# Another written-out order for a fused linear attention and squared-ReLU feed-forward kernel

## The chip, the cores and the metric

The kernel runs on one core of one Trainium2 chip. The metric is the time of one execution on the device in microseconds (us). Three runs of the kernel before gave 346.32, 346.35 and 348.3 us; their median is 346.35 us. Lower is better.

The core has five engines with queues of their own: PE (matmul; its weight loads are shown as PEld), DVE (vector), ACT (scalar, with the exponentials), POOL (here it issues the loads) and SP (here it issues transposes by DMA, and stores). Each works through its instructions strictly in the order in which the program lists them, so an instruction that waits holds up all that stand behind it on its engine.

## The reference

Two stages. The first is a linear attention with a feature map made of two exponentials, for 8 batches of 8 heads, 576 positions and 64 channels:

```python
def phi(x):
    proj = np.einsum('bhsd,df->bhsf', x, w_phi)
    proj = proj - np.max(np.abs(proj), axis=-1, keepdims=True)
    return np.concatenate([np.exp(proj), np.exp(-proj)], axis=-1)
q_p, k_p = (phi(q), phi(k))
kv = np.einsum('bhsf,bhsd->bhfd', k_p, v)
z = np.sum(k_p, axis=2)
num = np.einsum('bhsf,bhfd->bhsd', q_p, kv)
den = np.einsum('bhsf,bhf->bhs', q_p, z)[..., None] + 1e-06
return (num / den).astype(np.float32)
```

The second takes the result as 4608 tokens of 512 features, with w_in of 512x2048 and w_out of 2048x512:

```python
h = np.maximum(x @ w_in, 0.0)
return (h * h @ w_out).astype(np.float32)
```

## The kernel before, in words

The program first makes a list of 1741 operations (`add`, from line 60), each with an engine, a function that emits its instructions, and what it reads and writes. An operation is named here by its number in that list and its short name, as in 989:Xxk. Nothing of the list depends on the constants that the change touches.

For a batch b the operations are these. Loads of k, q and v by POOL (`xk` at L254, `xq` at L283, `xqr` at L274, `xv`; the last 64 positions at L262 as `xks`, `xqs`, `xvs`). Transposes of k and q: for batches 0 and 1 by PE (`Txk`, `Txq`, L325) with a copy out of PSUM (`Cxk`, `Cxq`), from batch 2 on by one DMA each from SP's queue (`Xxk`, `Xxq`, L336). The projection by w_phi in groups (`Pk`, `Pq`, L352, for batch 0 L379 and L501; `Fq`, L579, gives it the other way round). These have a contraction of 64 rows, so that two of them stand in the upper and lower half of PE's array at once; the list marks them `tiled`, and all other work of PE uses the full array. Then the greatest absolute value (`Mk`, `Mq`, on DVE), two exponentials (`Ekp`, `Ekn`, `Eqp`, `Eqn`, on ACT), the scaling of v (`em` on ACT, `V`, `V4` on DVE), `KV` on PE (L465, L470) and its copy `kvc`. For batches 3 to 7 the features of q are made row-wise and transposed by a DMA from SP (`Xf`, L558). The output of the attention for 128 positions is `NA`, a scaling `SA` on DVE, `NB` (L658), a reciprocal `rd` and a product `xo`; for the first 128 positions the same is done in two halves (`NAh`, `SAh`, `NBh`, `rdh`, `xoh`). It is transposed by PE for batch 0 (`Tx`, `Txh`, with the copies `Cx`, `Cxh`) and by a DMA from SP after that (`Xx`, L718).

The feed-forward works on chunks of 512 tokens. `F1` (L804; for the first chunk in smaller pieces at L815, L829 and L843) makes 4 matmuls of 128x512 into one PSUM bank, `relu` takes it out (on ACT at L781 or on DVE at L783), `sq` squares it (L790), `F2` (L898) makes 4 matmuls of 128x512 of a sum over 16, and `ot` copies the result, which SP stores. The last 128 tokens go in two parts (L862, `last_out`). The feed-forward of one chunk is mixed with the attention of the batches that come after it.

What sets the order is written out by hand in constants at the end of the file:

- `ORDER` (from L983) is a permutation of the 1741 operations. Each engine emits its own of them in this order; `pin` (L136) ties every instruction to the one before it on its engine.
- `STATES` gives one bit for each operation that can run on ACT or on DVE: the `relu`, `ot` and `kvc` operations and the copies of the transposes by PE.
- `BASES` gives the PSUM bank (0 to 7) of each of the 380 uses of a bank. A use waits until the one before it in the same bank has been read out.
- `GATES` names, for each load from batch 2 on, an operation of another engine that must have ended before the load is issued.
- `FILL` puts matmuls of zeros (128 wide, L977) ahead of some operations of PE in the first microseconds; nothing reads what they write.

The lines that use the constants:

```python
        if now[0].seq in GATES:
            dep(i, plan.ops[GATES[now[0].seq]].ins, mybir.DependencyClass.Sync)
...
        for op in self.ops:
            if op.alt is not None and STATES[op.group] == "1":
                op.eng, op.occ, op.lat = op.alt
        for g, b in zip(self.banks, BASES):
            g.base = int(b)
        return [self.ops[i] for i in ORDER]
...
            bank, n = FILL[op.seq]
            for _ in range(n):
                pin(nc.tensor.matmul(out=psum[:, bank, :P], lhsT=warm, rhs=warm, start=True, stop=True))
```

Of the kernel before, what the change touches and what calls it, by code (L numbers as in the profile page):

```python
# [108 lines left out]
def kernel(  # L109
# [964 lines left out]
)  # L1074
STATES = (
    '0101000100010000111100000010110000000010000000010101011000000001000000001111001000100000000001010000'
    '0100011000010000010000000000000101001010001101000001000100101000100111111000000100000010011010011111'
    '110001011000011111011110110100100'
)
GATES = {  # L1080
# [46 lines left out]
```

## Time and profile before

| what | value |
| --- | --- |
| three runs | 346.32, 346.35, 348.3 us (median 346.35) |
| the profiled execution's own time | 345.83 us |
| its span, first to last instruction | 344.0 us |
| granted PE clock | 1.000 |
| busy: PE, DVE, ACT, POOL | 335.8, 269.8, 231.3, 95.6 us |
| matmuls (fillers among them) | 3301 (91) |
| moved by DMA | 51.51 MB |

The span is 1.83 us shorter than the execution's own time, and that time is 0.52 us under the median of the three runs. In the busy shares a matmul counts from its start to a modelled end, and matmuls overlap: a 128x512 matmul is given as 379 ns, while a row of 16 of them ends 3.45 us after it began, which is 0.216 us from start to start. So PE's busy time says where PE stood still for long, and the starts of its matmuls say how well it was filled. "x8" in a line of the timeline means that eight instructions of a kind were merged into it; the first figure is the start, the second the length, and what stands in brackets is the idle time before it and what ended that.

### The profile page before, as it was taken

How to read it: one execution, taken by the hardware profiler on the slowest of the kernel's cores; microseconds unless marked ns; L12 is line 12 of the kernel's file. 1: busy time of each engine (PE TensorE's matmuls, PEld its weight loads, DVE VectorE, ACT ScalarE, POOL GpSimd, SP SyncE). 2: the span in 40 equal slices, each digit the busy share in tenths (PEclk: the TensorE clock that was granted, in tenths of full speed). 3: DMA queues.
4: the chain of work that ended last, by engine and by line, in shares of the span. 5: the costliest groups of instructions: out<-in, count | busy, mean ns of one | idle time of the engine just before them, and what ended most of it. 6: DMA issues, size and time to landing. Idle time of an engine off the chain costs nothing.

```text
span 344.0 us, 8335 instructions
## 1 busy us (share of the span) xinstructions
PE 335.8 (98%) x3301; PEld 188.8 (55%) x3301; DVE 269.8 (78%) x519; ACT 231.3 (67%) x436; POOL 95.6 (28%) x143
## 2 busy tenths in 40 slices
PE   8799999999999999999999999999999999999995
PEld 7678866545544555546545654455565444444443
DVE  5999998899899988798979897897996546863431
ACT  5999987699979798686888987977566402220120
POOL 8738360854620660104604060330000000000000
PEclk9999999999999999999999999999999999999999
DMA  9999999998999999999999999998864922000115
GB/s 130 176 203 195 202 172 164 159 160 166 163 178 214 179 163 232 163 191 183 158 211 142 216 169 215 162 157 183 162 125 105 158 82 71 0 2 35 56 37 149
DMA packets 142935, 51.51 MB, mean 150 GB/s; under 512 B 111472, under 2 KB 138416, under 8 KB 142896
## 3 DMA queue, kind: packets, MB, share of 16 engines
q1 hardware_dynamic: 97488, 32.35, 50.0%
q0 software_dynamic: 44960, 18.23, 48.4%
q8 instruction: 26, 0.43, 0.5%
q10 hardware_dynamic: 448, 0.39, 0.4%
q14 instruction: 13, 0.11, 0.1%
HBM read 36.73 MB, written 9.44 MB: 134 GB/s over the span
## 4 chain that ended last, share of the span: by engine, by line
PE 87%; ACT 5%; DMA 3%; DVE 1%; issue 1%; POOL 1%; SPq 1%; POOLq 0%; DVEq 0%; ACTq 0%
PE psum L898 34%; PE psum L804 30%; PE psum L658 6%; PE psum L352 5%; PE psum L465 4%; PE psum L843 2%; DMA kT<-xk 2%; ACT kn L394 1%; PE psum L829 1%; PE psum L815 1%; ACT qpn L594 1%; PE psum L862 1%; ACT kp L394 1%; DMA xT<-xo 1%; PE psum L470 1%
## 5 line engine op out<-in xcount | busy, mean ns | idle before, releaser
L898 PE MATMUL psum<-wout,h 128*128 128x512 bf16 x560 | 133.2, 379 | 0.0
L804 PE MATMUL psum<-xT,win 128*128 128x512 bf16 x448 | 105.3, 379 | 0.3 <-DMA xT<-xo 0.3
L781 ACT ACTIVATE hr<-psum 128x512 bf16<-128x512 f32 x104 | 60.4, 603 | 57.2 <-PE psum L804 45.2
L898 PEld LDWEIGHTS <-h 128*128 128x128 bf16 x560 | 50.8, 98 | 54.9 <-issue 0.5
L804 PEld LDWEIGHTS <-win 128*128 128x128 bf16 x512 | 47.6, 98 | 53.4 <-DMA xT<-xo 0.8
L790 DVE TENSOR_TENSOR h<-hr 128x512 bf16<-128x512 bf16 x144 | 56.6, 414 | 10.7 <-ACT hr L781 10.3
L554 ACT ACTIVATE qf<-psum 128x1024 bf16<-128x1024 f32 (+1 forms) x50 | 46.1, 938 | 13.8 <-PE psum L352 11.3
L405 DVE TENSOR_REDUCE mk<-psum 128x8 f32<-128x1024 f32 (+1 forms) x35 | 38.7, 1111 | 4.6 <-ACT kp L411 2.7
L783 DVE TENSOR_SCALAR hr<-psum 128x512 bf16<-128x512 f32 x40 | 26.9, 684 | 13.7 <-PE psum L804 13.1
L411 ACT ACTIVATE kn<-psum 128x1024 bf16<-128x1024 f32 (+1 forms) x35 | 32.7, 939 | 5.9 <-PE psum L352 4.2
L411 ACT ACTIVATE kp<-psum 128x1024 bf16<-128x1024 f32 (+1 forms) x35 | 32.9, 940 | 4.1 <-PE psum L352 2.4
L274 POOL DMA_DIRECT2D xq<-in_q_dram x24 | 17.4, 728 | 64.3 <-ACT hr L781 12.0
L670 DVE TENSOR_TENSOR psum<-psum,en 128x520 f32<-128x520 f32 (+1 forms) x39 | 27.4, 702 | 9.2 <-PE psum L658 5.5
L658 PEld LDWEIGHTS <-qpn 128*128 128x128 bf16 x624 | 27.2, 98 | 13.3 <-issue 1.4
L437 DVE TENSOR_TENSOR va<-xv,va 64x256 bf16<-64x256 bf16 (+2 forms) x66 | 29.8, 472 | 2.0 <-ACT va L429 1.1
L658 PE MATMUL psum<-kv,qpn 128*128 128x65 bf16 x624 | 30.4, 193 | 0.1
L541 DVE TENSOR_REDUCE mq<-psum 128x8 f32<-128x1024 f32 (+1 forms) x25 | 27.7, 1109 | 2.7 <-ACT qf L554 2.4
L594 ACT ACTIVATE qpn<-psum 128x1024 bf16<-128x1024 f32 (+1 forms) x30 | 27.2, 942 | 2.0 <-PE psum L579 1.1
L254 POOL DMA_DIRECT2D xk<-in_k_dram x27 | 19.9, 738 | 31.1 <-ACT hr L781 15.9
L684 DVE TENSOR_TENSOR xo<-psum,rden 128x512 bf16<-128x512 f32 (+1 forms) x39 | 26.6, 685 | 0.9 <-DMA xT<-xo 0.3
L254 POOL DMA_DIRECT2D xv<-in_v_dram x27 | 19.8, 741 | 14.4 <-PE psum L658 10.0
L195 ACT ACTIVATE ot<-psum 128x512 f32<-128x512 f32 x20 | 12.0, 598 | 12.8 <-PE psum L898 12.7
(81 smaller groups left out, 379.8 us busy)
## 6 DMA issues: line engine op xcount, KB each, us to landing
out_dram<-ot SPq DMA_DIRECT2D x32, 256.0 KB, 3.0
xk<-in_k_dram POOLq DMA_DIRECT2D x25, 128.0 KB, 5.9
xq<-in_q_dram POOLq DMA_DIRECT2D x24, 128.0 KB, 4.2
xv<-in_v_dram POOLq DMA_DIRECT2D x24, 128.0 KB, 4.9
win<-in_moe_w_in_dram POOLq DMA_DIRECT2D x4, 512.0 KB, 10.4
wout<-in_moe_w_out_dram POOLq DMA_DIRECT2D x4, 512.0 KB, 10.3
xq<-in_q_dram POOLq DMA_DIRECT2D x4, 256.0 KB, 5.9
out_dram<-ot SPq DMA_DIRECT2D x6, 128.0 KB, 2.6
```

The source lines that it names most:

```text
L254: pin(nc.gpsimd.dma_start(out=x[:, a * 512 : z * 512].rearrange("p (h x) -> p h x", x=4 * D), in_=src[b][2 * a : 2 * z, 0:512, :].rearrang ...
L405: pin(nc.vector.tensor_reduce(out=mk_view(g), in_=ps2(pj)[:, :, : n * Fd].rearrange("p e (i f) -> p e i f", f=Fd), axis=AX.X, op=ALU.max, ...
L411: pin(nc.scalar.activation(out=dst[slot][:, :, :n, :].rearrange("p e i f -> p e (i f)"), in_=ps2(pj)[:, :, : n * Fd], func=ACT.Exp, scale= ...
L437: pin(nc.vector.tensor_tensor(out=t[:, :, :D].rearrange("p m (x c) -> p m x c", c=2), in0=x.rearrange("p (m x c) -> p m x c", m=n, c=2), i ...
L541: pin(nc.vector.tensor_reduce(out=mqb[:, c, :, :n], in_=ps2(pj)[:, :, : n * Fd].rearrange("p e (i f) -> p e i f", f=Fd), axis=AX.X, op=ALU ...
L554: pin(nc.scalar.activation(out=o, in_=i_, func=ACT.Exp, scale=sgn))
L594: pin(nc.scalar.activation(out=o, in_=i_, func=ACT.Exp, scale=sgn))
L658: pin(nc.tensor.matmul(out=o[:, u // 4, u % 4 * D1 : (u % 4 + 1) * D1], lhsT=qpn[slot][:, sg * half + u * m : sg * half + u * m + P], rhs= ...
L781: pin(nc.scalar.activation(out=hr[sl], in_=ps1(g), func=ACT.Relu))
L790: pin(nc.vector.tensor_tensor(out=dst, in0=i_, in1=i_, op=ALU.mult))
L804: pin(nc.tensor.matmul(out=o, lhsT=win[mc // 4][:, kc, mc % 4 * P : (mc % 4 + 1) * P], rhs=x, start=(kc == 0), stop=(kc == KC - 1)))
L898: pin(nc.tensor.matmul(out=ps1(g), lhsT=h2[c % 2][mc // 4][:, mc % 4, tt * P : (tt + 1) * P], rhs=wout[mc // 4][:, mc % 4, :], start=(mc = ...
```

## The change

The five constants are replaced; not one operation is added, removed or altered, and every function of the program stays as it is. Cut to the lines that are spoken of (the first number of a line of `ORDER` has no meaning; the two lists are cut at other places by the line length alone):

```diff
 ORDER = [
-    2, 0, 6, 5, 8, 1, 7, 17, 10, 23, 13, 3, 4, 11, 15, 12, 16, 44, 45, 14, 46, 18, 49, 47, 77, 88, 48, 78, 20, 89,
-    50, 79, 52, 22, 90, 83, 85, 21, 94, 96, 51, 19, 84, 91, 53, 66, 30, 92, 113, 80, 54, 32, 82, 67, 55, 114, 95, 24,
...
-    345, 216, 183, 350, 397, 173, 217, 184, 174, 185, 383, 205, 218, 340, 346, 351, 189, 341, 190, 206, 186, 342,
...
-    302, 520, 280, 398, 202, 257, 303, 521, 273, 283, 258, 274, 295, 281, 269, 255, 284, 526, 256, 275, 285, 399,
...
-    307, 379, 315, 308, 548, 316, 309, 584, 317, 400, 404, 403, 552, 392, 406, 401, 318, 322, 556, 420, 395, 323,
...
-    499, 731, 540, 493, 656, 494, 749, 495, 626, 459, 655, 628, 753, 500, 618, 657, 620, 622, 609, 754, 665, 621,
-    623, 501, 612, 735, 502, 503, 611, 710, 666, 773, 714, 625, 736, 793, 610, 668, 706, 627, 667, 677, 702, 707,
...
-    964, 826, 697, 950, 827, 907, 842, 951, 698, 908, 968, 699, 700, 862, 969, 874, 828, 916, 877, 909, 989, 903,
-    875, 911, 904, 830, 843, 925, 876, 832, 905, 899, 701, 865, 829, 912, 939, 831, 926, 864, 833, 917, 900, 866,
-    913, 921, 863, 929, 922, 901, 927, 855, 867, 918, 886, 1367, 923, 991, 970, 947, 930, 993, 985, 934, 940, 992,
...
+    2, 0, 1, 17, 12, 6, 7, 5, 15, 23, 3, 9, 11, 16, 10, 4, 14, 44, 45, 13, 46, 18, 49, 47, 88, 77, 48, 89, 22, 78,
+    90, 52, 20, 51, 79, 96, 30, 95, 66, 85, 83, 113, 21, 53, 93, 91, 19, 50, 80, 92, 34, 114, 54, 8, 84, 67, 55, 25,
...
+    212, 223, 358, 268, 389, 377, 252, 244, 251, 383, 259, 224, 512, 361, 247, 388, 249, 372, 250, 301, 292, 254,
+    593, 302, 362, 248, 253, 516, 363, 261, 272, 303, 201, 391, 367, 520, 262, 398, 386, 293, 202, 257, 378, 387,
...
+    276, 319, 392, 306, 277, 320, 544, 321, 399, 534, 307, 278, 370, 282, 281, 308, 313, 400, 314, 538, 401, 315,
...
+    600, 653, 599, 495, 731, 654, 458, 604, 499, 735, 792, 626, 500, 620, 656, 745, 624, 628, 655, 501, 736, 749,
+    502, 622, 503, 657, 609, 665, 610, 753, 668, 720, 754, 633, 612, 621, 724, 666, 719, 1170, 611, 706, 1168, 635,
...
+    813, 825, 698, 950, 821, 831, 815, 699, 830, 843, 700, 862, 951, 989, 874, 863, 907, 876, 903, 833, 877, 832,
+    911, 864, 908, 952, 929, 820, 701, 904, 819, 912, 917, 865, 913, 970, 899, 855, 875, 866, 921, 900, 909, 905,
+    930, 925, 901, 922, 918, 826, 926, 990, 931, 886, 991, 927, 834, 992, 828, 827, 1014, 994, 923, 836, 867, 835,
...
 BASES = (
-    '4646164041135252302126010200212463200564360250721353062204415777202261022550062627452774740476572002'
...
+    '3027061374341562122716452046650406464142600425321445456663272342324066466020444001720131014535316624'
...
 STATES = (
-    '0101000100010000111100000010110000000010000000010101011000000001000000001111001000100000000001010000'
...
+    '0101010000000000100001010101000000000000000001100100011000100010010000001000001101110000100101110100'
...
 GATES = {
-    380: 186, 381: 90, 382: 144, 383: 53, 384: 344, 385: 119, 386: 93, 387: 361, 388: 44, 389: 65, 390: 339, 391: 67,
...
+    380: 184, 381: 194, 382: 228, 383: 371, 384: 197, 385: 149, 386: 218, 387: 248, 388: 91, 389: 359, 390: 340,
...
 FILL = {
-    44: (0, 26), 46: (0, 6), 79: (0, 2), 53: (0, 21), 55: (7, 6), 68: (7, 4), 109: (7, 3), 119: (7, 13),
-    150: (5, 10),
+    44: (0, 26), 46: (0, 8), 88: (1, 3), 90: (5, 4), 79: (7, 3), 66: (7, 2), 55: (0, 9), 119: (4, 15), 175: (4, 2),
+    147: (3, 9), 122: (2, 2), 129: (2, 3), 164: (7, 3),
 }
```

Counted over the whole of both lists: of the `relu` operations 40 run on DVE before and 43 after, of the `ot` 15 and 14, of the `kvc` 14 and 13, of the copies of transposes of k and q 13 and 14; the others run on ACT. Fillers are 91 before and 89 after. In the list of PE's operations, two neighbours of which one is `tiled` and the other isn't stand 106 times before and 96 times after.

More of the change, by code (lines that the diff above doesn't have):

```diff
@@ L983 @@
 ORDER = [
[84 rows of a table removed]
[84 rows of a table added]
 ]
 BASES = (
-    '4646164041135252302126010200212463200564360250721353062204415777202261022550062627452774740476572002'
-    '2234050406562660306644747744515564044733360014606323030002065257723721523632167404444060644135642622'
-    '2411755603017321744466422012226426662113311032101300001014426622554324066124147766101100154152402636'
-    '46617631044214100632037002065360056746106374667253600175114302553045653704562301'
+    '3027061374341562122716452046650406464142600425321445456663272342324066466020444001720131014535316624'
+    '4520364044000426664070736120063336252744040462213026664622422123033100210163010444200415230026066377'
+    '7545641626501273542622036766404000606044212567775273246764206432626002404400220011211063002331736464'
+    '65454024020022027334724675357666454352233772216364547742253770443765767176405332'
 )
 STATES = (
-    '0101000100010000111100000010110000000010000000010101011000000001000000001111001000100000000001010000'
-    '0100011000010000010000000000000101001010001101000001000100101000100111111000000100000010011010011111'
-    '110001011000011111011110110100100'
+    '0101010000000000100001010101000000000000000001100100011000100010010000001000001101110000100101110100'
+    '1101000000000001111000010010010100000001011100000000010001001001001101001000100001011000001011011000'
+    '111100101010101110001100001011001'
 )
 GATES = {
[11 rows of a table removed]
[11 rows of a table added]
 }
 FILL = {
-    44: (0, 26), 46: (0, 6), 79: (0, 2), 53: (0, 21), 55: (7, 6), 68: (7, 4), 109: (7, 3), 119: (7, 13),
-    150: (5, 10),
+    44: (0, 26), 46: (0, 8), 88: (1, 3), 90: (5, 4), 79: (7, 3), 66: (7, 2), 55: (0, 9), 119: (4, 15), 175: (4, 2),
+    147: (3, 9), 122: (2, 2), 129: (2, 3), 164: (7, 3),
 }
```

168 rows, old and new, of tables (GATES, ORDER) are left out of this document.

## The prediction

> **What bounds the kernel now.** I read the page's busy shares and slices first, then busy time by stretches, then PE's waits, and last the timeline where PE waits or changes its kind of work. From the page:
>
> ```profile
> PE 335.8 (98%) x3301; PEld 188.8 (55%) x3301; DVE 269.8 (78%) x519; ACT 231.3 (67%) x436; POOL 95.6 (28%) x143
> ...
> PE   8799999999999999999999999999999999999995
> ...
> DVE  5999998899899988798979897897996546863431
> ACT  5999987699979798686888987977566402220120
> ...
> q8 instruction: 26, 0.43, 0.5%
> ```
>
> PE is the bound from the second slice on; DVE and ACT are as full as PE only in the first slices. By stretches (span, then busy time of PE, PEld, DVE, ACT, POOL, then granted clock and DMA):
>
> ```profile
> 0.00:27.00 27.00, 23.07 (x348) 18.40 (x349) 23.01 (x56) 22.70 (x51) 17.57 (x29) 1.00 1.31 171
> 27.00:45.00 18.00, 17.98 (x292) 15.51 (x290) 17.22 (x34) 17.26 (x35) 10.28 (x15) 1.00 1.39 198
> 45.00:245.00 200.00, 199.48 (x2052) 107.97 (x2050) 174.16 (x320) 161.65 (x300) 67.73 (x100) 1.00 1.24 178
> 245.00:344.00 99.00, 95.27 (x616) 46.89 (x614) 55.45 (x112) 29.68 (x54) 0.00 (x0) 1.00 0.33 78
> ```
>
> Standing still, PE loses 3.93 us before 27 us, 0.5 us from there to 245 us, and 3.7 us at the end, where the last copy and store follow the last matmul. Of the waits after the head, two are on DMAs:
>
> ```profile
> PE psum L804 <- DMA xT<-xo: 0.3, 1, 0.3
> ...
> PE psum L352 <- DMA kT<-xk: 0.2, 1, 0.2
> ```
>
> These are understated, since a matmul is shown busy past its streaming. From start to start it is more:
>
> ```profile
> 107.87 0.59 PE L804 MATMUL psum<-xT,win 128*128 128x512 bf16 x2
> ...
> 108.79 0.39 PE L804 MATMUL psum<-xT,win 128*128 128x512 bf16 x1 [0.32 <-DMA xT<-xo]
> ```
>
> Two matmuls begin at 107.87 and, 0.22 later, 108.09; the third should follow at 108.30 and begins at 108.79, 0.49 late. In the same way the `Pk` at 154.07 us, which waits for kT, is 0.33 late.
>
> Last, what a change of kind costs PE:
>
> ```profile
> 68.69 1.04 PE L898 MATMUL psum<-wout,h 128*128 128x512 bf16 x4
> 69.66 0.40 PE L352 MATMUL psum<-wphi,qT 64*128 64x128 bf16 x8
> 69.89 0.38 PE L579 MATMUL psum<-qT,wphi 64*128 64x512 bf16 x2
> 70.14 0.40 PE L352 MATMUL psum<-wphi,qT 64*128 64x128 bf16 x8
> 70.47 0.39 PE L804 MATMUL psum<-xT,win 128*128 128x512 bf16 x1
> ```
>
> Four `F2` matmuls take 4 x 0.216 = 0.86 us, but from 68.69 to the half-array matmuls at 69.66 pass 0.97. Eight of those take 0.23 when half-array work follows (69.66 to 69.89) and 0.33 when full-array work does (70.14 to 70.47). So each passage between the kinds costs about 0.10 us, both ways, and no row of waits shows it.
>
> With starts, the whole sum closes: the useful matmuls at their spacing (0.216 us for 512 wide, 0.109 for 256, 0.056 for 128, 0.029 for 65, half that for half-array pairs) make 313 us. The first useful one starts at 4.1 us, the last at 340.05. The 23 us between are 106 passages (10 us), some 10 us of fillers and waiting up to 27 us, and some 3 us of small delays after that, 2.8 of them from 45 to 245 us.
>
> **The change part by part.** The sum is made against the profiled execution's 345.83 us (span 344.0, and 1.83 around it).
>
> Passages: 106 become 96. Ten at 0.10 us make -1.0 us. Every one lies on PE's own row, where nothing covers it. The order of `Pk`, `Pq` and `Fq` decides alone, so I take the whole; 0 and -1.0 are the ends.
>
> The Trainium skill ("TensorE: Matmul & The Clock Gate", Part 2, step 1) says that PE pulls the loading of the next weights ahead of matmuls in flight when their row groups don't conflict or they go to the background buffer. Read alone, that would hide the passage and make this term 0, which is a rival below. The 0.10 us at 69.66 and 70.47 speak against it.
>
> The two DMA waits. I laid the useful matmuls at their spacing, plus passages, between an operation's place in ORDER and its first user on PE. From 495:Xx to the first `F1` of its chunk (710 before, 720 after) lie 2.6 us of PE work before and 5.4 after. It landed 3.3 us after its issue, so the wait of 0.49 is gone. From 989:Xxk to 991:Pk it is 7.1 before and 8.0 after; the 0.9 more exceed the 0.33 that it came late. The other transposes keep a least distance of 4.6 us for `Xx` (2.6 before), 7.0 for `Xf` (6.5) and 8.0 for `Xxk` (7.1). What is late next is 1476:Xx (4.6, landing after 2.4) and 885:Xx (4.9, landing after 3.1), both with room. I take -0.8; ends -0.8 and 0.
>
> The head, which is PE's place only in name. From 5.9 to 25 us DVE's instructions follow each other without a gap over 0.12 us, and ACT's too; PE waits for them. ACT has the same load ahead of the last `kvc` before the output (132): copies 110 and 208 leave it, 78 and 226 come, of the same size. On DVE, ahead of 144:xoh, four copies of kT go (three of 128x512 at 415 ns, one of 128x256 at 273, each starting some 0.08 before the one before has ended: 1.2 us) and two copies of qT and a memset (410, 410, 278 ns: 0.95) come, -0.25. But between 144 and the copies `Cxh` that give the feed-forward its first input now stand 118 and 210, +0.5. So `Cxh` (25.73 and 25.94) ends some 0.3 later. PE meanwhile does `Pq`, `Fq` and `Pk` (1.1 us) that it did around the first `F1` pieces anyway, so only part of the delay reaches it. The start is bound by the landing of k at 3.70 us (ACT's cast) and 5.97 us (the load that is issued first in both), so the earlier identity on POOL gains nothing. I take +0.2. Ends: -1.0, about a third of the 2.9 us that PE idles there after its first filler, and +0.9, the 1.2 us that DVE would lose if the moved copies waited for PE as 45 and 47 did (0.89 and 0.85 idle), less 0.3.
>
> Fillers: 91 become 89, in time in which PE waits for DVE and ACT; 0. If that cover is gone they cost 89 x 0.056 = 5 us, as now.
>
> Engines: three more `relu` on DVE (684 ns; ACT 603), one `ot` and one `kvc` fewer, one copy more, about +1.4 us on DVE and as much less on ACT. DVE idles 25.8 us between 45 and 245; 0, at worst +0.5 in the head's last part.
>
> Banks, other small delays: banks are used again no sooner than before (0.86 us of PE work after the matmul that filled them, in both, outside the head); before, such waits cost 0.15 to 0.18 each, four times. 0; ends -0.5 and +1.0. The last operations of PE and the stores stand in the same order: 0.
>
> Loads on POOL: the second block of keys is issued after as much data as before (8.3 MB, 8.5 before, by the sizes of the page's list of DMA issues), but planned later; 0, with its danger below.
>
> Sum: 345.83 - 1.0 - 0.8 + 0.2 = 344.2. The median of the runs stood 0.5 over the profiled time, so 344.7 us, 1.6 us or 0.5% under 346.35. A measurement of this kernel tells about 1% (3.5 us) from no change.
>
> **The rivals.**
>
> Slower: the keys come late. 383:xk, a quarter of batch 2's keys, must land before 398:Xxk, which must land before 400:Pk. Between lay 16.2 + 11.6 us of PE work, now 4.3 + 10.9 = 15.2. Loads of keys take 5.9 us to land and these transposes 6.2 (medians), 12.1 together, and it holds. But 383 itself took 9.7, since twelve loads stood in the queue, and the longest transpose 8.3: 18.0, so PE would stand 2.8 us, and everything behind 398 on SP (two `Xx`, then the transpose of q) with it: 347.5. POOL issued these loads up to 3.7 us late before; with that too, 351.2. From a wait of 1.7 us on the result is slower than before. Against it: the queue's content ahead of 383 isn't greater.
>
> Gains beyond the sum: the head shortens by 1.0 and all 2.8 us of small delays vanish: 345.83 - 1.0 - 1.0 - 2.8 + 0.5 = 341.5. For it: the DMA distances grew nearly everywhere. Against: the head's load on DVE and ACT is the same.
>
> It doesn't do what it says: other operations take the late places, only the passages are saved and the head gives them back: 346.3.
>
> The clock: the first 26 fillers start 0.108 us apart (26 in 2.95 us, the last lasting 0.25), the 21 at 7.63 us 0.056. So PE has a half rate, though the granted clock reads 1.00 there. That block of 21 becomes blocks of 3, 2 and 9. If PE fell to half rate from 9.0 to 26.9 us, its 10.4 us there would be 20.8; 17.9 less 10.4 and ten passages leave 6.5, so 3.9 late: 348.6. Against it: no idle time in the head exceeds 1.0 us.
>
> The passages are free: were the weights of the next kind loaded behind the running matmuls everywhere else, the ten passages fewer would bring nothing, and the sum would be 345.7. For it: PEld is busy for half of PE's time only. Against it: the five rows above, both ways.
>
> **How the numbers follow.** Forecast 0.60 (343.5 to 345.6); beyond the sum 0.11; keys late 0.10; nothing gained 0.11; passages free 0.04; clock 0.04. The range leaves out most of the second (342.6 and less) and the worse half of keys late with the clock (over 347.6): 342.6 to 347.6. Faster by over 1% (under 342.9) is most of the second case, 0.09; slower by over 1% (over 349.8) the bad end of keys late and part of the clock, 0.05; within, 0.86.
>
> **What would show it.** Right: no wait of PE on xT near 108 us or on kT near 150; a first `F1` piece at 27 to 28 us; starts with ten fewer passages; a span near 342.4. Wrong: a wait of PE on kT near 60 us; fillers at 0.108 after 9 us; idle time of PE over 4 us before 27 us; or many new short waits for `relu` between 45 and 245 us.

## The result and the profile after

The changed kernel takes 349.95 us (median of 11 runs, 348.4 to 351.49); the kernel before took 346.7 us beside it (11 runs, 346.16 to 348.35). The ratio is 1.0081, 95% interval 1.0054 to 1.0108: slower by 0.8%, where 0.5% faster was forecast. The profiled execution took 348.46 us (span 346.3), the second fastest of its 11 runs; that of before took 345.83 (span 344.0). Ratios below are to the kernel before, run beside each experiment. Runs more than 1.5% above the fastest run of their kernel are left out of the ratios (six of e2's twelve, three each of f2's and f6's, at most two of any other kernel); over all runs the medians of e2, f2 and f6 stand at 1.0075, 1.0039 and 1.0074.

The page of the changed kernel, the lines that answer to those of before:

```profile
PE 335.0 (97%) x3299; PEld 188.3 (54%) x3299; DVE 271.1 (78%) x521; ACT 232.2 (67%) x434; POOL 95.5 (28%) x143
...
PE   7889899999999999999999999999999999999995
...
q8 instruction: 26, 0.43, 0.5%
```

Its busy time by stretches, with the same columns as before:

```profile
0.00:27.00 27.00, 22.48 (x334) 17.13 (x335) 22.95 (x56) 22.70 (x51) 19.91 (x32) 1.00 1.28 154
27.00:45.00 18.00, 16.49 (x286) 14.52 (x285) 16.03 (x33) 15.97 (x31) 6.39 (x9) 1.00 1.36 199
45.00:245.00 200.00, 198.35 (x2029) 108.37 (x2027) 176.84 (x323) 160.47 (x292) 67.83 (x100) 1.00 1.21 178
245.00:346.30 101.30, 97.65 (x654) 48.26 (x652) 55.28 (x113) 33.01 (x61) 1.41 (x2) 0.99 0.38 81
```

PE stands still for 4.52 us before 27 us (3.93 before the change), 1.51 us from there to 45 (0.02) and 1.65 us from 45 to 245 (0.52). The middle is where a kernel bound by PE may not lose, and it loses there at few places. From PE's waits (us in total, times, longest):

```profile
PE psum L829 <- DMA win<-in_moe_w_in_dram: 1.5, 1, 1.5
PE psum L465 <- DVE va L437: 1.4, 2, 0.7
...
PE psum L325 <- DMA xk<-in_k_dram: 1.0, 2, 0.8
...
PE psum L658 <- DVE mq L541: 0.5, 1, 0.5
PE psum L352 <- DVE xo L684: 0.4, 1, 0.4
```

The two waits that were to go, on xT at 109 us and on kT at 154, are not among them. What stands there in their place I followed in the timeline.

**At 36 us, a load.** PE reaches the fourth quarter of w_in before the load 29:win has landed:

```profile
35.51 0.40 PE L352 MATMUL psum<-wphi,kT 64*128 64x128 bf16 x8
35.74 0.28 PE L352 MATMUL psum<-wphi,qT 64*128 64x128 bf16 x4
35.85 0.27 PE L579 MATMUL psum<-qT,wphi 64*128 64x256 bf16 x2
37.64 1.07 PE L829 MATMUL psum<-xT,win 128*128 128x128 bf16 x16 [1.51 <-DMA win<-in_moe_w_in_dram]
```

From start to start that is 1.59 us late: where the load holds up nothing, the last row follows 0.20 us after the one before it (e1 below), not 1.79. 29:win was issued at 23.44 us and landed at 37.59; in the kernel before it was issued at 17.66, landed at 29.89 and was needed at 34.64.

**At 84 us, another load.** One of the two waits on `va` L437 stands there:

```profile
85.65 0.19 PE L465 MATMUL psum<-va,kn 128*128 128x65 bf16 x1 [0.75 <-DVE va L437]
```

From start to start the operation 434:KV loses 1.1 us in two places. It waits for DVE's 430:V and 431:V; 430 began at 83.97 us behind 393:xv, landed at 83.87.

**At 171 and 175 us, banks.** PE, then ACT, DVE and SP of the changed kernel, in separate views:

```profile
171.53 0.41 PE L658 MATMUL psum<-kv,qpn 128*128 128x65 bf16 x8 [0.51 <-DVE mq L541]
...
175.80 0.40 PE L352 MATMUL psum<-wphi,kT 64*128 64x128 bf16 x8 [0.35 <-DVE xo L684]
```

```profile
168.28 1.94 ACT L554 ACTIVATE qf<-psum 128x1024 bf16<-128x1024 f32 x2 [1.28 <-DMA qpn<-qf]
```

```profile
170.26 1.23 DVE L541 TENSOR_REDUCE mq<-psum 128x8 f32<-128x1024 f32 x1 [1.00 <-ACT qf L554]
...
175.05 0.69 DVE L684 TENSOR_TENSOR xo<-psum,rden 128x512 bf16<-128x512 f32 x1 [0.90 <-DMA xT<-xo]
```

```profile
159.95 4.64 SPq L558 DMA_TRANSPOSE qpn<-qf  x1
...
165.30 2.24 SPq L558 DMA_TRANSPOSE qpn<-qf  x1
167.64 9.32 SPq L718 DMA_TRANSPOSE xT<-xo  x4
```

Read from PE backwards: 880:NA waits for a PSUM bank; 1036:Mq on DVE, the last to read that bank, waits until 1038:Eqn and 1037:Eqp on ACT have read it; 1038 writes a buffer that 878:Xf, a transpose on SP, still reads (issued at 159.95, landed at 168.18). At 175 us the same by another way: 884:xo writes the buffer of 849:Xx, issued at 168.92 behind 890:Xf and landed at 174.96. In both places what PE lacks is a bank, and what keeps the bank is an operation waiting for a transpose to let go of its input.

In the kernel before the maximum comes first and the exponentials behind it, and `NA` waits for neither (DVE, ACT and PE, in separate views):

```profile
167.47 1.22 DVE L541 TENSOR_REDUCE mq<-psum 128x8 f32<-128x1024 f32 x1
```

```profile
168.83 1.92 ACT L554 ACTIVATE qf<-psum 128x1024 bf16<-128x1024 f32 x2
```

```profile
169.25 0.41 PE L658 MATMUL psum<-kv,qpn 128*128 128x65 bf16 x8
```

The banks differ too. By the two lists, 880:NA takes the banks of 1007:Pk in the kernel before and those of 1035:Pq in the changed one, each time 4.0 us of PE's work after they were filled. So as much work as before lies between, but the bank is now one that 1036, 1037 and 1038 have to read out.

Start to start, laid against the useful matmuls and 0.094 us for a passage, the changed kernel is behind the one before by 0.59 us at the first `F1` piece, 2.15 after the load at 36 us, 3.5 after 84 us, 2.55 at 170 us (it gains 0.5 at 109 us and 0.3 at 154, the two waits that went), 3.86 at 176 us and 3.32 at the end. Ten passages fewer give 0.94 back: 2.4 us, of which the spans show 2.3.

### The profile page after: what moved, and what is told of

Same layout as the page of the kernel before. It is cut to its first block, busy times and chain, and to the rows that moved or that the text cites. A ratio compares the mean times of both kernels' runs of the same rounds, so it can differ in the third digit from the quotient of the medians.

```text
span 346.3 us, 8299 instructions
## 1 busy us (share of the span) xinstructions
PE 335.0 (97%) x3299; PEld 188.3 (54%) x3299; DVE 271.1 (78%) x521; ACT 232.2 (67%) x434; POOL 95.5 (28%) x143
## 4 chain that ended last, share of the span: by engine, by line
PE 81%; DMA 11%; POOL 4%; ACT 1%; DVE 1%; issue 1%; SPq 0%; POOLq 0%; DVEq 0%; ACTq 0%
PE psum L898 33%; PE psum L804 29%; PE psum L658 5%; PE psum L352 4%; PE psum L465 4%; DMA win<-in_moe_w_in_dram 4%; DMA xq<-in_q_dram 3%; DMA xv<-in_v_dram 2%; PE psum L843 2%; DMA xT<-xo 2%; PE psum L862 1%; PE psum L470 1%; POOL xq L283 1%; POOL xk L254 1%; PE psum L579 1%
## 5 line engine op out<-in xcount | busy, mean ns | idle before, releaser
L898 PE MATMUL psum<-wout,h 128*128 128x512 bf16 x560 | 133.4, 379 | 0.0
L781 ACT ACTIVATE hr<-psum 128x512 bf16<-128x512 f32 x101 | 58.0, 597 | 56.7 <-PE psum L804 36.6
L898 PEld LDWEIGHTS <-h 128*128 128x128 bf16 x560 | 51.3, 98 | 56.3 <-issue 0.2
L783 DVE TENSOR_SCALAR hr<-psum 128x512 bf16<-128x512 f32 x43 | 29.1, 686 | 17.5 <-PE psum L804 16.7
L437 DVE TENSOR_TENSOR va<-xv,va 64x256 bf16<-64x256 bf16 (+2 forms) x66 | 30.2, 472 | 3.7 <-ACT va L429 1.6
L541 DVE TENSOR_REDUCE mq<-psum 128x8 f32<-128x1024 f32 (+1 forms) x25 | 27.8, 1112 | 5.7 <-PE psum L352 2.9
```

The source lines that it names most:

```text
L437: pin(nc.vector.tensor_tensor(out=t[:, :, :D].rearrange("p m (x c) -> p m x c", c=2), in0=x.rearrange("p (m x c) -> p m x c", m=n, c=2), i ...
L541: pin(nc.vector.tensor_reduce(out=mqb[:, c, :, :n], in_=ps2(pj)[:, :, : n * Fd].rearrange("p e (i f) -> p e i f", f=Fd), axis=AX.X, op=ALU ...
L781: pin(nc.scalar.activation(out=hr[sl], in_=ps1(g), func=ACT.Relu))
L783: pin(nc.vector.tensor_scalar(out=hr[sl], in0=ps1(g), scalar1=0.0, scalar2=None, op0=ALU.max))
L898: pin(nc.tensor.matmul(out=ps1(g), lhsT=h2[c % 2][mc // 4][:, mc % 4, tt * P : (tt + 1) * P], rhs=wout[mc // 4][:, mc % 4, :], start=(mc = ...
```

## The experiments

Theory 1: the new order needs some loads sooner than POOL's queue brings them. Theory 2: it is the order of copies in the head. Theory 3, formed after the first runs: between 145 and 176 us operations that must wait for a transpose stand ahead of operations that free a bank for PE. In several of these traces one `F2` record in each of 32 places is missing (528 of 560), shown as up to 1.3 us of "issue" on L898; those are no waits.

### e1: one load earlier

```diff
 POOL: 26:win 27:win 28:win
+29:win
 33:xq 38:xvs 35:xqs 43:wout
-29:win
 41:wout
```

> The changed kernel (349.95 us, 1.0081 of before) with one load moved: 29:win, the last quarter of w_in, is issued right behind 28:win instead of behind four other loads (33, 38, 35, 43). Theory 1 (the loss is loads that land too late for the new order): 29:win landed at 37.59 us and its first user on PE began then, 1.67 us late; the load now lands near 33 us and the 1.67 us go: 348.3 us, 1.0033 of before. Risk: 33:xq lands some 2.5 us later, and it had 2.8 us to spare. Theory 2 (the loss is the order of the copies on DVE and ACT in the head, and banks): the piece that waited for 29:win would next wait for something else, and the time stays at 349.95, 1.008.

Measured: 1.0035 (1.001 to 1.006), 348.62 us. PE's row at the same place:

```profile
36.07 0.28 PE L352 MATMUL psum<-wphi,qT 64*128 64x128 bf16 x4
36.19 0.27 PE L579 MATMUL psum<-qT,wphi 64*128 64x256 bf16 x2
36.39 1.07 PE L829 MATMUL psum<-xT,win 128*128 128x128 bf16 x16
```

29:win now lands at 32.11 us, the wait is gone, and nothing takes its place nearby. Theory 1 names the right size here. But in this trace PE then waits at 175.54 us for 884:xo, 1.26 us from start to start where the changed kernel's own trace had 0.50.

### e2: 393:xv earlier

```diff
 POOL: 590:xv 578:xk
+393:xv
 586:xqr 584:xqr 588:xqs 785:xqs 395:xv 583:xqr
-393:xv
```

> The changed kernel with another load moved: 393:xv, a quarter of batch 2's v, is issued right behind 578:xk instead of as the last of that batch, eight loads later. Theory 1: 393 landed at 83.87 us, DVE's 430:V began at 83.97 and two KV on PE stood 1.1 us behind it; that goes: 348.8 us, 1.0050 of before. Theory 2: 430:V would be held by the work ahead of it on DVE, and no more than 0.2 us are won: 1.0075.

Measured: 1.0015 (0.9976 to 1.0053); the median of all its runs is 350.28 us. It settles nothing by itself. In e6, which has the same move, 393 lands at 75.48 us, and no `KV` waits at 84 us. That does not end the matter: 395:xv is then the last of the batch's v, and in f6, which has the move too, it landed at 83.56 us (79.12 in the changed kernel) and cost PE more than 393 had (below).

### e4: one transpose earlier

```diff
 SP: 878:Xf 916:st
+849:Xx
 890:Xf 873:Xx
-849:Xx
 861:Xx
```

> The changed kernel with one transpose moved on SP: 849:Xx stands ahead of 890:Xf, not two places behind it. Its input was ready at 161.35 us, it was issued at 168.92 and landed at 174.96, and 884:xo on DVE began 0.1 us later, with two Pk on PE (0.51 us late at 175.2 us) behind it. Theory 1b (SP's transposes are late for the new order in one place): the transpose lands near 172 us, 884:xo begins at about 174.2 and the 0.5 us go: 349.4 us, 1.0066 of before. Theory 2b (the two Pk wait for banks for another reason): nothing is won, 1.008.

Measured: 1.0044 (1.0023 to 1.0066). 849 lands at 169.17 us, 884:xo begins at 174.04 and the two `Pk` no longer wait; 880:NA is 0.70 late, as in the changed kernel (0.67), and at 211.89 us a wait of 1.02 us for an `ot` on DVE is new. The gain is nearer to 0.4% than to the 0.15% expected, though the interval reaches to that.

### e6: four moves, and no gain

The moves of e1, e2 and e4, and 16:xk ahead of 23:xq at the start.

> The changed kernel with four moves at once: 29:win behind 28:win, 393:xv behind 578:xk, 849:Xx ahead of 890:Xf, and 16:xk ahead of 23:xq at the start (16:xk landed at 8.86 us and PE's 66:Txk, 0.93 us late, began 0.05 later). Theory 1: 1.67 + 1.1 + 0.5 go, and of the 0.9 at the start about 0.4 reaches PE's first feed-forward matmul: 346.3 us, 0.999 of before, and the ten passages fewer begin to show. Theory 2: the head stays as it is since DVE and ACT bind there, and half of the rest turns into other waits: 348.5 us, 1.005.

Measured: 1.0059 (1.0025 to 1.0092). The 0.999 of theory 1 is out. The 1.005 of theory 2 lies inside the interval, but what the trace shows is only in part the head. PE's waits:

```profile
PE psum L658 <- DVE mq L541: 1.3, 1, 1.3
...
PE psum L804 <- ACT hr L781: 1.0, 1, 1.0
```

The two loads and 849 wait no longer, and after the head and up to 145 us PE loses no more than in the kernel before. Then 899:F1 is 1.16 us late at 150.63, for the bank of 904:relu, which stands on ACT behind 864:Eqp, which waits for 842:Xf (landed 148.97); and 880:NA is 1.49 late at 171.98 in the way told above. The swap of the first two loads cost 0.9 us in the head, since 23:xq then kept a transpose of q waiting. In the kernel before, 904 stands ahead of 864, 1036 ahead of 1038, and 849 ahead of 890. That is theory 3.

### f1: three turns back, no load moved

```diff
 ACT: 
+904:relu
 864:Eqp
-904:relu
 ...
 DVE and ACT:
+1036:Mq
 1038:Eqn 1037:Eqp
-1036:Mq
 ...
 SP:
+849:Xx
 890:Xf 873:Xx
-849:Xx
```

> The changed kernel with all loads in its own order and three operations put back on the side on which the kernel before has them: 904:relu ahead of 864:Eqp on ACT, 1036:Mq on DVE ahead of 1038:Eqn on ACT, 849:Xx ahead of 890:Xf on SP. In each place something waited for the reading of a buffer by one of SP's transposes (842:Xf, 878:Xf, 849:Xx) and PE waited for a PSUM bank behind it. Theory 3 (a second cause beside the loads: from 145 to 176 us an operation that must wait for a transpose to have read its buffer stands ahead of one that frees a bank for PE): PE lost 1.2 us there in the profiled run of the changed kernel, 1.3, 4.4 and 2.7 us in three of the runs since; these go, and the ratio falls from 1.0081 to about 1.003 (348.0 us where before takes 347). Theory 1 alone (only the late loads): no change, 1.008.

Measured: 1.0006 (0.9978 to 1.0034), 347.69 us. Theory 3 holds, with more than it promised: the interval lies wholly below that of the changed kernel, though that kernel was run in another round and each ratio is to the kernel before in its own. ACT and DVE of this kernel:

```profile
147.85 0.60 ACT L781 ACTIVATE hr<-psum 128x512 bf16<-128x512 f32 x1
148.32 1.96 ACT L554 ACTIVATE qf<-psum 128x1024 bf16<-128x1024 f32 x2
...
167.93 1.94 ACT L554 ACTIVATE qf<-psum 128x1024 bf16<-128x1024 f32 x2 [1.74 <-DMA qpn<-qf]
```

```profile
166.25 1.23 DVE L541 TENSOR_REDUCE mq<-psum 128x8 f32<-128x1024 f32 x1 [0.78 <-PE psum L352]
```

ACT still waits for the transpose, 1.74 us, longer than before. Now the relu and the maximum are done by then, and PE does not wait with it. It waits a little later, 0.69 and 0.35 us from start to start at 172 us, for work on DVE that the earlier 1036 pushed back (it passes four operations there). So between 145 and 176 us this trace loses 1.04 us, against 1.21 in that of the changed kernel, which was one of its fastest runs. The two traces do not show where the 2.6 us between the ratios went. What speaks for the turns is the runs themselves, the 2.65 us that e6's trace lost in the same stretch, and r1.

### r1: four such turns made in the kernel before

```diff
 ACT:
+864:Eqp
 904:relu
 ...
-864:Eqp
 ...
+888:Eqp
 940:relu
 ...
-888:Eqp
 ...
 DVE and ACT:
+1038:Eqn
 1036:Mq
 ...
-1038:Eqn
 ...
 SP:
+890:Xf
 849:Xx
-890:Xf
```

> The kernel before with three of its turns made as in the changed kernel: 864:Eqp ahead of 904:relu and 888:Eqp ahead of 940:relu on ACT, 1038:Eqn on ACT ahead of 1036:Mq on DVE. Banks and all else are its own. Theory 3: 904, 940 and 1036 then wait for the transposes 842, 866 and 878 (landed at 148.4, 156.6 and 167.4 us in its profile; the three began at 147.7, 154.9 and 167.5), and PE behind them by about 1 us each where the bank that they free is needed next: 1.003 to 1.009 of before. If the turns alone cost nothing without the changed kernel's banks and transposes: 1.000.

Measured: 1.0077 (1.0047 to 1.0107), 350.37 us. Loads, banks and engines are those of the kernel before, and a loss as large as that of the change is there. The expectation leaves out the turn on SP, which the kernel has as well; 849 landed at 172.07 us, 3.7 ahead of 884:xo, so no wait comes from it in this trace. ACT of the kernel before at the two relus, then ACT of this one, then its PE:

```profile
147.68 0.60 ACT L781 ACTIVATE hr<-psum 128x512 bf16<-128x512 f32 x1 [0.49 <-PE psum L804]
```

```profile
154.89 0.59 ACT L781 ACTIVATE hr<-psum 128x512 bf16<-128x512 f32 x1
```

```profile
149.50 1.02 ACT L554 ACTIVATE qf<-psum 128x1024 bf16<-128x1024 f32 x1 [1.59 <-DMA qpn<-qf]
150.42 0.59 ACT L781 ACTIVATE hr<-psum 128x512 bf16<-128x512 f32 x1
...
158.72 0.60 ACT L554 ACTIVATE qf<-psum 128x512 bf16<-128x512 f32 x1 [1.34 <-DMA qpn<-qf]
159.22 0.59 ACT L781 ACTIVATE hr<-psum 128x512 bf16<-128x512 f32 x1
```

```profile
151.06 1.02 PE L804 MATMUL psum<-xT,win 128*128 128x512 bf16 x4 [0.98 <-ACT hr L781]
152.72 3.61 PE L804 MATMUL psum<-xT,win 128*128 128x512 bf16 x16 [0.64 <-DVE kv L193]
...
159.86 0.19 PE L465 MATMUL psum<-va,kp 128*128 128x65 bf16 x1 [1.36 <-ACT hr L781]
```

In the kernel before the two relus began at 147.68 and 154.89 us and the exponentials behind them; here each relu has to wait until the exponential's buffer is free, and PE stands idle for 0.98, 0.64 (by way of DVE, which waits for work that stands behind 904 on ACT) and 1.36 us behind them. The turn of 1038 and 1036 costs PE nothing here: 880:NA takes another bank. So r1 shows that such turns cost what the change lost, but not that they cost it at the same places: 940 is none of f1's three, and at 1036 and 849 this trace loses nothing. That 1.0077 comes so near to 1.0081 is in part chance, since r1 has neither the late loads nor the fewer passages.

### f2, f3: turns and loads together

f2 has the turns of f1, the loads of e1 and e2, and 383:xk ahead of 389:xqr. f3 adds 940:relu ahead of 888:Eqp (a fourth such place) and 1004:Mk behind 881:SA.

> The same three turns, and three loads earlier: 29:win behind 28:win, 393:xv behind 578:xk, 383:xk ahead of 389:xqr (383 landed 0.05 to 0.1 us before it was needed, and PE waited 0.5 and 0.6 us for its transpose in two runs). If the late loads (2.8 us together) and the three turns (1.2 us and more) are the whole loss, the ten passages fewer and the two waits that went are what is left: 0.995 of before. If the head, which is 0.6 to 0.9 us longer, counts in full too: 0.998. If new waits take their place, as in the run with four moves: 1.003 or more.

> The three turns and the three earlier loads, and two more turns: 940:relu ahead of 888:Eqp on ACT, the fourth place where an exponential that must wait for a transpose (866:Xf) to have read its buffer stands ahead of a relu that frees a bank (PE lost 2.04 us there in the profiled run of the kernel with turns and loads); and on DVE 1004:Mk behind 881:SA, since the earlier 1036:Mq had pushed 881 0.7 us late. Theory 3 (such turns and the late loads are the whole loss): 2 us less there, 1 us less at 172 us, 0.994 to 0.997 of before, and runs that scatter less than the 345.3 to 352.1 us of the kernel without these two. If the scatter has another source: 1.000.

Measured: f2 1.0007 (0.9967 to 1.0047), f3 1.0002 (0.9975 to 1.003). The loads add nothing to the turns that can be measured. In f2's trace PE lost 2.04 us (start to start) at the fourth place:

```profile
PE psum L804 <- ACT hr L781: 1.9, 1, 1.9
```

f3's profiled run took 345.98 us. There PE was 0.98 us ahead of the kernel before at 168 us, the ten passages and nothing else, and then gave 1.2 back at 171 to 173 us, waiting for 1112:ot and for an exponential.

### f4, f5, f6: what was left to try

f4 is f3 with 139:Cxh ahead of 118 and 210 on DVE; 146:Cxh, which its expectation names too, stayed behind them. f5 is f3 with 1004:Mk behind 1112:ot as well. f6 is f3 with 1036 and 1004 in the changed kernel's places.

> The same kernel, and in the head on DVE the copies 139:Cxh and 146:Cxh, which give the feed-forward its first input, ahead of the copies 118:Cxq and 210:Cxq of transposes of q, not behind them. If the two copies of q on DVE are what made the head late (Cxh ended 0.8 us later than in the kernel before, the first F1 piece began 1.2 us later): the first piece begins 0.4 us earlier and the time falls by 0.3 us. If what follows is bound by the exponentials on ACT: no change.

> The kernel with four turns and three earlier loads, and 1004:Mk on DVE put behind 1112:ot, not only behind 881:SA: PE's 1153:F2 waited 0.78 us at 171 us for the bank that 1112:ot frees. Theory: the 0.78 us go and 1005:Ekp, which waits for 1004, comes 0.7 us later, which costs PE's 1047:Pq up to that. Between 0 and -0.8 us: 0.998 to 1.000 of before.

> The changed kernel with the three earlier loads and the turns of 904, 940 and 849, but 1036:Mq and 1004:Mk left where the changed kernel has them. If the turn of 1036 only moved the loss from 880:NA (0.7 to 1.5 us late) to 882:NB and 1153:F2 (1.0 to 1.2 us late): about the same as with all turns, 1.000 of before. If that turn is a gain: 1.003.

Measured: 1.0028 (0.9999 to 1.0058), 1.0034 (1.0005 to 1.0063), 1.0025 (0.999 to 1.0061). None is better than f3. In f4 139 began at 26.55 us, no sooner than the 26.53 of f3, since DVE stood idle for 0.59 us until PE had its input ready; 146 began at 27.40, not 26.85, and the first `F1` piece at 28.56, not 28.09. So the two copies do not hold up 139; whether they hold up 146 was not tried, and theory 2 was not put to the test as meant. f6, whose expectation was 1.000 or 1.003, doesn't tell the two apart. Its profiled run took 350.55 us and lost most at a place that has nothing to do with 1036 (DVE, then PE):

```profile
83.68 0.69 DVE L437 TENSOR_TENSOR va<-xv,va 128x1024 bf16<-128x1024 bf16 x1 [3.19 <-DMA xv<-in_v_dram]
```

```profile
86.27 1.15 PE L804 MATMUL psum<-xT,win 128*128 128x512 bf16 x4 [2.68 <-ACT hr L781]
```

DVE's 439:V waits for 395:xv, squares stand behind it on DVE, a relu on ACT waits for those, and PE lacks the relu's bank: 2.85 us from start to start. 395 took 9.5 us to land here and 5.8 in f3's trace, with the same order on POOL.

### e5: the late load alone, in the kernel before

```diff
 POOL: 27:win 28:win 26:win
-29:win
 36:xqs 33:xq 382:xk 38:xvs 39:xvs 40:wout 41:wout
+29:win
```

> The kernel before with one load moved: 29:win behind 41:wout, seven loads later, about as late as in the changed kernel. Theory 1: it lands near 37.6 us, where the fourth quarter of w_in was needed at 34.64 us: PE waits 3 us there, the time rises by as much, to 1.0085 of before. If such a wait is made good later, because PE's later waits shrink: 1.003 or less.

Measured: 1.0191 (1.0159 to 1.0223), +6.6 us at a median of 347.3 beside it (the medians alone lie 7.2 us apart). The load landed at 41.52 us, later than meant, since POOL's queue stood at 382:xk for its gate:

```profile
41.57 1.03 PE L829 MATMUL psum<-xT,win 128*128 128x128 bf16 x8 [5.60 <-DMA win<-in_moe_w_in_dram]
```

5.6 of the 6.6 us are this wait. Here a wait of PE at 36 us reaches the end in full; nothing later makes it good.

### p_fewer, p_more, p_more_small: what a passage is worth

The kernel before with other places for groups of `Pk`, `Pq`, `Fq`: 92, 144 and 134 passages in place of 106. In p_more_small the last of a group goes behind the next full-array operation, 14 times:

```diff
 PE:
-794:Pk
 764:F1
+794:Pk
```

> The kernel before with its order of loads, banks and engines, and eight of its groups of matmuls moved past a neighbouring group, so that PE changes between half-array and full-array work 92 times, not 106. At 0.094 us for a passage: 1.3 us less, 0.996 of before. If the passages cost nothing beside what else PE waits for: 1.000. Risk: the moved matmuls are up to 2 us later or earlier for those who wait for them.

> The kernel before with 19 groups of half-array matmuls split by one full-array operation (an F1 or F2 of four matmuls that stood beside the group), so that PE changes its kind of work 144 times, not 106. At 0.094 us for a passage: 38 x 0.094 = 3.6 us more, 1.010 of before. If the passages are free: 1.000.

> The kernel before with 14 groups of half-array matmuls split by moving the last of the group behind the next single F1 or F2 (0.86 us later), so that PE changes its kind of work 134 times, not 106. At 0.094 us for a passage: 28 x 0.094 = 2.6 us more, 1.0076 of before, and no new wait of PE over 0.3 us. If the passages are free: 1.000.

Measured: p_fewer 1.0212 (1.0164 to 1.0261), p_more 1.0243 (1.0207 to 1.0279), p_more_small 1.0137 (1.0103 to 1.017). All three are slower than expected, the one with fewer passages most against it. In PE's waits of p_fewer stand what the moves cost:

```profile
PE psum L352 <- ACT kp L411: 2.9, 2, 1.9
PE psum L352 <- DVE mq L508: 1.7, 2, 0.9
...
PE psum L658 <- ACT qpn L594: 1.0, 1, 1.0
...
PE psum L352 <- ACT qf L554: 1.0, 1, 1.0
```

The group that was moved came to a bank that was still being read. The passage itself kept its price in every trace: from start to start, after 45 us, the median is 0.095 to 0.096 us into half-array work and 0.092 out of it, in the kernel before, the changed one and all three of these. In p_more_small 28 passages at 0.094 make 2.6 us and seven new waits (0.33 to 0.70 us, start to start) 3.05; together that is 5.7, where the profiled run's span is 6.3 us longer and the runs show 4.75. So a passage is about a tenth of a microsecond, and moving one operation by 0.86 us cost some 0.22 on average in this trace (3.05 over 14 moves), as much as the two passages that it made. By the Trainium skill, "TensorEngine Tiling (Array Packing)", Tiling Modes, Key Properties, a change of tiling mode drains TensorE; the time lost on both sides, 0.095 and 0.092 us, agrees with that, though no trace here shows the draining itself.

### g1: the two transposes of the kernel before

```diff
 SP:
+495:Xx
 540:st
-495:Xx
 ...
+989:Xxk
 916:st
-989:Xxk
```

> The kernel before with two transposes on SP put ahead of the store that stands before each: 495:Xx ahead of 540:st and 989:Xxk ahead of 916:st. Each is then issued 0.6 to 0.8 us earlier, and the two waits of PE in its profile, 0.49 at 109 us and 0.33 at 154 us, shrink or go: -0.8 us, 0.9977 of before. If other waits take their place: 1.000.

Measured: 0.9999 (0.997 to 1.0029). Nothing to be seen of 0.8 us; the interval holds it.

No version beat the kernel before by more than its interval. The nearest are f1 and f3, at 1.0006 and 1.0002.

## Why the prediction was wrong

- **Passages, -1.0.** Right in the trace: ten fewer, 0.094 us each. The rival that they are free is out. (At the spacings given there the useful matmuls come to about 310 us, not 313; the forecast does not use that sum.)
- **Two DMA waits, -0.8.** They went, and the two traces close up by 0.5 and 0.3 us at those places. What that brings over many runs is below what g1 could show.
- **The step that failed: "The other transposes keep a least distance ... both with room", and with it "Banks, other small delays: 0".** I measured from each transpose to the first reader of its output on PE. A transpose has another follower, the next writer of its input buffer: `Eqp` and `Eqn` for `Xf`, `xo` for `Xx`. These wait on ACT and DVE, and I did not ask what stands behind them there. In the kernel before, 849:Xx landed 4.0 us ahead of 884:xo, 878:Xf 1.4 ahead of its exponential, 866:Xf 1.0; in the changed one 0.1 each. And where the kernel before has a relu or a maximum first and the waiting exponential second, the changed one has them turned. I said that banks were used again no sooner than before, in PE's work. That was nearly so (outside the head at the least 0.67 us, 0.81 before, in one place each), but who frees them had moved. The runs put 0.75% on the three turns (1.0081 to 1.0006), 2.6 us where I had 0 with an end at +1.0; r1 loses 0.77% by turns of this kind in the kernel before, 904's at a place that is also f1's, 940's at one that is not. The five kernels built on these turns with other moves (f2 to f6) lie between 1.0002 and 1.0034.
- **"Loads on POOL ... 0."** Mis-sized too: 1.6 us at 36 us, 1.1 at 84 us in the trace, 0.46% in e1. I compared how much data stood ahead of the keys and did not do the same for w_in. The rival "keys late" had the mechanism and the wrong load: 398:Xxk landed at 62.52 us for a `Pk` at 62.57, and in the traces of e1, e4, f1 and f4 PE waited 0.5 to 0.6 us there. (When 383 was issued in the kernel before, seven loads had not landed; twelve is the number that shared its 9.7 us.)
- **The head, +0.2.** It was +0.6, inside its ends; the first `F1` piece began at 28.08 us, not at 27 to 28.
- **The clock rival** is out: the fillers after 9 us stand 0.055 us apart.
- **The signs.** Idle time before 27 us of 4.52 us had been named as a sign of failure, and so had waits for relus. In the profiled run, one of the fastest, there were none of the latter over 0.3 us; they came in the traces of e6, f2 and r1.

What stays open: turns and loads together (f2, f3) bring no more than the turns alone, though each trace shows the load's wait gone. PE then comes sooner to the stretch after 145 us (f2 has the same work done at 141.5 us as the changed kernel at 144.1) and meets transposes that do not land as much sooner; that is argued from single traces and was not shown. Nor is it known why the runs of these kernels scatter by up to 8 us (f3: 345.98 to 353.64) where the kernel before keeps to 345.3 to 350.9. A part of it can be read: f3 and f6 have one order on POOL, and the landing of 395:xv alone put 2.85 us between their traces. Theory 2 is open, since f4 made only half of its move: the first `F1` piece is 0.6 us behind, and no run shows by what.

## What to carry to other kernels

When an order is changed, follow each DMA to both of its ends: the reader of what it writes, and the next writer of what it reads. On a queue that works strictly in order, put what frees a PSUM bank ahead of what may wait for a DMA, and judge a distance by the longest landing time in the trace, not by the one of that transfer. A saving of a tenth of a microsecond per passage is worth having only where the group can move without meeting a bank that is still being read.

## What the runs showed of the hardware

**A load is not issued before the one eight places ahead of it has landed.** POOL of the changed kernel:

```profile
16.11 0.61 POOL L262 DMA_DIRECT2D xk<-in_k_dram  x1 [2.04 <-DMA xk<-in_k_dram]
...
27.77 0.74 POOL L303 DMA_DIRECT2D wout<-in_moe_w_out_dram  x1 [2.79 <-DMA win<-in_moe_w_in_dram]
30.34 0.88 POOL L254 DMA_DIRECT2D xv<-in_v_dram  x1 [1.82 <-DMA win<-in_moe_w_in_dram]
```

The loads eight places ahead landed at 15.83, 27.49 and 30.06 us, each 0.28 before. The kernel before has the same 0.28 (20:xv landed at 12.19, 34:xq issued at 12.47), and in neither trace is a load issued sooner after that landing. Whether the chip or the program's semaphores set this the runs do not tell. So a load that comes late holds up all that POOL has still to issue; that 30:xk landed only at 15.83 is one of the delays behind 29:win's issue at 23.44.

**Transposes of one shape land after very different times.** In the changed kernel 878:Xf took 8.2 us from issue to landing, 842:Xf 4.5; 849:Xx took 6.0 and 885:Xx 2.4. The order around them must stand the longer.

**Two engines read one bank in turn.** 1036:Mq on DVE began 0.04 us after 1037:Eqp on ACT had ended, though its input was ready 3 us earlier. The Trainium skill ("PSUM — Partial Sum Buffer", PSUM bank collisions raise a hardware error) says that the compiler's scheduler puts a dependency between any two instructions of different engines on the same bank and quadrant, reads included; the row agrees, and it is what lets a late exponential hold a maximum that has all that it needs.
